# The loads of w1, 32 x 512 KB, are issued from ScalarE's DMA queue instead of SyncE's

## Chip, cores and metric

The kernel runs on one core of a Trainium2 chip. The metric is device time in microseconds (us); less is better. A core has five engines that each work through their own list of instructions: TensorE (PE), VectorE (DVE), ScalarE (ACT), GpSimd (POOL) and SyncE (SP), which here does nothing but issue loads and stores. They wait for one another by semaphores. A load is issued by an engine's sequencer (written SPq or ACTq in the profile) and moved by 16 DMA engines.

## What is computed

Three stages, float32. Windowed attention over 4 x 8 heads, 576 positions, head size 64, of which each position sees itself and the 63 before it; its result as 2304 tokens of 512; a soft mixture of 8 experts with 4 slots each; and a layer with softplus.

```python
scores = scale * np.matmul(q, k.transpose(0, 1, 3, 2))
mask = (rel >= 0) & (rel < window)                 # window = 64
x = softmax(scores where mask) @ v                 # 2304 x 512
...
logits = x @ phi                                   # 2304 x 32 slots
d = np.exp(logits - logits.max(0)); d /= d.sum(0) + 1e-09
slot_input = d.T @ x                               # 8 experts x 4 slots x 512
h = np.maximum(slot_input[e] @ w1[e], 0.0)         # w1: 8 x 512 x 1024
slot_out[e] = h @ w2[e]                            # w2: 8 x 1024 x 512
c = np.exp(logits - logits.max(1)); c /= c.sum(1) + 1e-09
x = c @ slot_out
...
h = x @ w_in                                       # 512 x 2048
g = np.maximum(h, 0.0) + np.log1p(np.exp(-np.abs(h)))
return g @ w_out                                   # 2048 x 512
```

## The kernel before

**Attention.** The 2304 tokens are 18 tiles of 128. Each tile t has a load of q (`do_lq`), of k (`do_lk`) and of v (`do_lv`), 256, 256 and 260 KB, into rings of four buffers. TensorE makes the scores (S, L227), VectorE masks them and finds the maxima (T, L238), GpSimd subtracts (M, L245), ScalarE takes exponentials (E, L248), TensorE transposes (PT, L254), ScalarE or VectorE copies the transposes out of PSUM (PC, by `evac`, L195), TensorE multiplies with v (PV, L272), VectorE normalises. Every four tiles the logits are made and folded into a running softmax over the tokens; ScalarE's part of that begins with the copy `lt` (L314).

**Weights.** w1 is 32 tiles of 128 x 1024 floats, 512 KB each, loaded by `load_w1` (L144 to L147) into 32 buffers that no one used before, so no load of w1 waits for a buffer. They are needed when the attention is over, by the first expert layer (`emit_l1`, L582). w2 is 32 more such tiles for the second expert layer (`emit_l2`, L625), loaded by `load_w2` (L156): the first four into space that the q and k buffers leave (`do_cl`, after the scores of the last tile), seven into what the other attention buffers leave, the rest into buffers of w1 as the first expert layer has used them. Behind w2 come w_in and w_out in halves of the last layer (L693, L696), which runs from about 130 us to the end.

**What sets the order.** A planner in the program, `arrange`, gets a table of steps with costs, dependencies and due times, and emits their instructions in the order that it finds. Loads are steps of the planned engine Q:

```python
step_1(("LQ", t), dict(Q=0.67), [("S", t - NQB)])
step_1(("LK", t), dict(Q=0.67), [("S", t - NKB + 1)])
step_1(("LV", t), dict(Q=0.67), [("PV", 2 * (t - NVB) + 1), ("VD", t - NVB + 1)])
...
step_1(("LW", j), dict(Q=1.31), [("LW", j - 1)], goal=100.0)
...
step_1(("CL", n), dict(Q=0.01), [("S", 17), ("LW", N1 - 1)] if n == 0 else [("PV", 35), ("CL", 0), ("VD", 17)])
```

So w1 (LW) is laid between the loads of q, k and v, two per tile, with a late due time. In the emitted program each engine keeps the order of emission. All loads share eight completion semaphores, DMAHW0 to DMAHW7, handed out in turn in the order of the program whatever engine issues; a load waits until the previous user of its semaphore, eight loads earlier, has landed. At the beginning ScalarE issues two loads itself, the first k tile and the constants.

Of the kernel before, what the change touches and what calls it, by code (L numbers as in the profile page):

```python
# [27 lines left out]
NWC0, NWC1 = 4, 7  # L28
NLAST, NEARLY = 2, 1
NWC = NWC0 + NWC1 + 3  # L30

# [72 lines left out]
def block_kernel(ctx: ExitStack, tc: tile.TileContext, q, k, v, phi, w1, w2, w_in, w_out, cst, out):  # L106
    nc = tc.nc
# [14 lines left out]
    def wtile(name):  # L122
        n_wt[0] += 1
        return (odd[n_wt[0] // 2 % 16] if n_wt[0] % 2 else wpa).tile([128, 1024], F32, tag="w", name=name)
# [18 lines left out]

    def load_w1(e, kt):  # L144
        t = wtile("w1t")
        nc.sync.dma_start(out=t, in_=w1[e, 128 * kt:128 * kt + 128, :])
        w_tiles["w1", e, kt] = t  # L147

    def load_w2(j, ts=None):
# [61 lines left out]
    def do_w1(e, j):  # L211
        load_w1(*w1_order[j])
# [338 lines left out]
    with tc.manual_schedule():  # L551
# [17 lines left out]
        l1_ps, h1_t, ring = {}, {}, {}  # L569
        takers = [NWC, "hTz0", NWC + 1, "hTz1"] + list(range(NWC + 2, NWC + 8))  # L570
        takers += [NWC + 8, "cc0", NWC + 9, "cc1", NWC + 10, "cc2"] + list(range(NWC + 11, N2 - NLAST))
        takers += [None] * (32 - len(takers))
# [30 lines left out]
        def emit_h1t(grp):  # L603
            h1 = h1_t.pop(grp)
            for hh in range(2):
                pst = bank(4 + hh, "ht_ps")
                for f in range(4):
                    base = h1[hh][:, 256 * (f // 2) + f % 2:256 * (f // 2) + f % 2 + 1]
                    rows = bass.AP(tensor=base.tensor, offset=base.offset, ap=[list(base.ap[0]), [2, 128]])
                    nc.tensor.transpose(pst[:, 128 * f:128 * f + 128], rows, ident)  # L610
                for e2 in range(2):
                    c0 = 16 * grp + 72 * e2
                    src0 = pst[:, c0:c0 + 1]
                    src = bass.AP(tensor=src0.tensor, offset=src0.offset, ap=[list(src0.ap[0]), [128, 4], [36, 2], [1, 4]])
                    dst0 = hTz[2 * grp + e2][:, 0, 4 * hh, 16 * grp + 8 * e2:16 * grp + 8 * e2 + 1]
                    dst = bass.AP(tensor=dst0.tensor, offset=dst0.offset, ap=[list(dst0.ap[0]), [NS, 4], [8 * NS + 4, 2], [1, 4]])
                    nc.vector.tensor_copy(dst, src)
# [3 lines left out]
        def emit_l2(j):  # L621
            e, r = w2_order[j]
            if r % 2:
                for g in range(4):
                    nc.tensor.matmul(  # L625
                        l2_ps[32 * g:32 * g + 32, :], hTz[e // 2][:, e % 2, 2 * r - 2 + g, :],
                        w_tiles["w2", j - 1 + g // 2][g % 2],
                        start=e == 0 and r == 1, stop=e == NE - 1 and r == 3,
                    )
# [16 lines left out]
        for i in range(4):  # L646
            t = ring[f"hTz{i // 2}"][:, 512 * (i % 2):512 * (i % 2) + 512]
# [25 lines left out]
        emit_h1t(1)  # L673
        for j in range(8, NWC):
            emit_l2(j)
# [52 lines left out]

        for j in range(NWC, N2):
            emit_l2(j)  # L730
            b, odd_j = divmod(j - NWC - 3, 2)
            if not odd_j and 0 <= b < 5:
# [288 lines left out]
```

## Time and profile before

| | us |
|---|---|
| median of 3 runs (lowest, highest) | 376.08 (375.13, 377.34) |
| the profiled execution, device time | 374.22 |
| its span, first to last instruction | 372.4 |
| TensorE busy | 361.5 (97%) |
| VectorE, ScalarE, GpSimd busy | 274.3, 236.7, 91.8 |
| moved on q1 (SP's queue) | 69.09 MB |
| moved on q10 (ScalarE's queue) | 0.66 MB |

The profile is one execution, a little shorter than the median run. Busy time is a share over stages with different limits, so the rows further down are taken by stage: attention until about 90 us, the expert layers until about 130 us, the last layer after that. In rows of the trace an arrow `out<-in` names what an instruction writes and reads, and `x2` counts instructions that one row stands for.

### The profile page before, as it was taken

What the parts mean: (1) busy time and instruction counts of PE and PEld (TensorE: products, weight loads), DVE (VectorE), ACT (ScalarE), POOL (GpSimd) and SP (SyncE); (2) the same over time, 40 slices, a digit from 0 to 9 for tenths busy, and PEclk for the clock granted to TensorE, in tenths of its full rate; (3) what the DMA queues carried; (4) which work ended last, traced back from release to release, by engine and by line L of the source; (5) the groups of instructions that cost most, each with busy time, mean ns of one, the idle gap of its engine ahead of it and who ended that gap; (6) DMA issues with size and microseconds to landing.
All of it is one profiled execution on the core that took longest, in us unless ns stands there. A gap on an engine that the chain in (4) does not pass through costs nothing.

```text
span 372.4 us, 8154 instructions
## 1 busy us (share of the span) xinstructions
PE 361.5 (97%) x3026; PEld 267.9 (72%) x3026; DVE 274.3 (74%) x777; ACT 236.7 (64%) x463; POOL 91.8 (25%) x111
## 2 busy tenths in 40 slices
PE   8999999998999998999999999999999999999995
PEld 6887878775333275887788878887768887878884
DVE  2786878845430399899998889989999885766562
ACT  1577665664200169888996687888778936666660
POOL 1999777730310001221000110122400100001230
PEclk9999999999999999999999999999999999999999
DMA  8999999999999994225330133141100030200222
GB/s 300 325 388 395 397 393 398 405 406 407 398 410 404 391 345 149 89 64 163 120 114 2 56 116 111 37 134 56 56 2 0 2 114 0 94 21 33 80 87 84
DMA packets 31096, 70.27 MB, mean 189 GB/s; under 512 B 2768, under 2 KB 11088, under 8 KB 31056
## 3 DMA queue, kind: packets, MB, share of 16 engines
q1 hardware_dynamic: 30768, 69.09, 50.4%
q10 hardware_dynamic: 288, 0.66, 0.5%
q8 instruction: 24, 0.39, 0.4%
q14 instruction: 16, 0.13, 0.1%
HBM read 65.02 MB, written 4.72 MB: 187 GB/s over the span
## 4 chain that ended last, share of the span: by engine, by line
PE 86%; DVE 5%; DMA 3%; ACT 2%; POOL 2%; issue 1%; DVEq 0%; POOLq 0%
PE y_ps L875 18%; PE y_ps L876 18%; PE y_ps L877 18%; PE x_ps L272 5%; PE s_ps L227 4%; PE pt_ps L254 4%; PE l_ps L582 4%; DMA w2t<-w_d 3%; PE x_ps L846 3%; PE xt_ps L295 2%; PE l_ps L625 2%; PE h_ps L846 2%; POOL sm L245 1%; PE lt_ps L305 1%; PE warm_ps L140 1%
## 5 line engine op out<-in xcount | busy, mean ns | idle before, releaser
L875 PE MATMUL y_ps<-whi,gh 128*128 128x512 f32 x288 | 115.1, 400 | 0.4 <-DVE part L886 0.3
L876 PE MATMUL y_ps<-wlo,gh 128*128 128x512 f32 x288 | 114.4, 397 | 0.0
L877 PE MATMUL y_ps<-whi,gl 128*128 128x512 f32 x288 | 113.7, 395 | 0.4 <-DVE gl L765 0.4
L765 POOL TENSOR_TENSOR gl<-g,gh 128x384 fp32r<-128x384 f32 (+2 forms) x24 | 26.9, 1119 | 225.0 <-DVE gh L762 126.5
L875 PEld LDWEIGHTS y_ps<-whi,gh 128*128 128x128 f32 x288 | 54.1, 188 | 16.5 <-issue 2.1
L877 PEld LDWEIGHTS y_ps<-whi,gl 128*128 128x128 f32 x288 | 54.1, 188 | 13.8 <-DVE gl L765 1.2
L876 PEld LDWEIGHTS y_ps<-wlo,gh 128*128 128x128 f32 x288 | 54.1, 188 | 11.1
L854 ACT ACTIVATE a<-a 128x512 f32<-128x512 f32 (+2 forms) x81 | 47.4, 585 | 2.6
L853 ACT ACTIVATE a<-a 128x512 f32<-128x512 f32 (+2 forms) x81 | 47.4, 586 | 1.5
L238 DVE CUSTOM_DVE_ANT_0 sm<-s_ps,cst_sb 128x128 f32<-128x128 f32 x144 | 32.8, 286 | 12.4 <-PE s_ps L227 8.9
L245 POOL TENSOR_TENSOR sm<-mx,sm 128x512 f32<-128x512 f32 x36 | 36.9, 1036 | 15.8 <-DVE mx L238 11.3
L765 DVE TENSOR_TENSOR gl<-g,gh 128x512 fp32r<-128x512 f32 (+1 forms) x57 | 36.9, 648 | 2.5 <-ACT gh L762 0.6
L849 ACT ACTIVATE a<-x_ps 128x512 f32<-128x512 f32 (+2 forms) x50 | 27.1, 547 | 16.4 <-PE x_ps L846 12.9
L858 DVE SCALAR_TENSOR_TENSOR g<-x_ps,a 128x512 f32<-128x512 f32 (+2 forms) x50 | 31.3, 627 | 7.3 <-ACT a L854 2.9
L762 DVE CAST gh<-g 128x512 fp32r<-128x512 f32 (+2 forms) x59 | 23.1, 391 | 13.9 <-PE y_ps L876 13.3
L248 ACT ACTIVATE sm<-sm 128x512 f32<-128x512 f32 x36 | 22.6, 634 | 16.9 <-POOL sm L245 16.3
L849 ACT ACTIVATE a<-h_ps 128x512 f32<-128x512 f32 (+1 forms) x31 | 16.9, 550 | 21.1 <-PE h_ps L846 21.1
L195 ACT COPY pt<-pt_ps 128x512 f32<-128x512 f32 x33 | 18.4, 584 | 6.8 <-PE pt_ps L254 6.7
L858 DVE SCALAR_TENSOR_TENSOR g<-h_ps,a 128x512 f32<-128x512 f32 (+1 forms) x31 | 19.6, 633 | 4.1 <-ACT a L854 3.4
L272 PE MATMUL x_ps<-vd,pt 128*64 128x65 f32 x288 | 21.6, 225 | 0.7 <-DVE xn L287 0.4
L272 PEld LDWEIGHTS x_ps<-vd,pt 128*64 128x64 f32 x288 | 18.5, 137 | 4.8 <-issue 3.1
L272 PE MATMUL x_ps<-vt,pt 128*64 128x65 f32 x288 | 21.7, 226 | 0.0
(143 smaller groups left out, 537.7 us busy)
## 6 DMA issues: line engine op xcount, KB each, us to landing
w1t<-w_d SPq DMA_DIRECT2D x32, 512.0 KB, 7.5
w2t<-w_d SPq DMA_DIRECT2D x29, 512.0 KB, 10.2
wi<-w_in_d SPq DMA_DIRECT2D x16, 512.0 KB, 5.3
wo<-w_out_d SPq DMA_DIRECT2D x16, 512.0 KB, 3.5
vt<-v_d SPq DMA_DIRECT2D x18, 260.0 KB, 6.0
qb<-q_d SPq DMA_DIRECT2D x18, 256.0 KB, 5.7
out_d<-o SPq DMA_DIRECT2D x18, 256.0 KB, 2.0
kr<-k_d SPq DMA_DIRECT2D x17, 256.0 KB, 5.8
```

Source lines behind the costliest of these rows:

```text
L238: nc.vector.tensor_tensor_reduce(out=sm[:, p], in0=ps[:, 128 * p:128 * p + 128], in1=mask, scale=-0.125, scalar=3.0e38, op0=ALU.add, op1=A ...
L245: nc.gpsimd.tensor_tensor(out=sm_t[i], in0=mb, in1=sm_t[i], op=ALU.subtract)
L272: nc.tensor.matmul(x_ps[64 * par:64 * par + 64, a, 65 * p:65 * p + 65], pt[:, 128 * p + 64 * par:128 * p + 64 * par + 64], vt[:, 65 * h:65 ...
L762: (nc.scalar.copy if e == "A" else nc.vector.tensor_copy)(dst, src)
L765: eng[e].tensor_tensor(out=dst, in0=a, in1=b.bitcast(F32), op=ALU.subtract)
L849: nc.scalar.activation(out=st["a", i], in_=st["h", i], func=AF.Abs)
L853: nc.scalar.activation(out=a, in_=a, func=AF.Exp, scale=-1.0)
L854: nc.scalar.activation(out=a, in_=a, func=AF.Ln, bias=1.0)
L858: nc.vector.scalar_tensor_tensor(out=st["g", i], in0=st["h", i], scalar=0.0, in1=st["a", i], op0=ALU.max, op1=ALU.add)
L875: nc.tensor.matmul(y, st["gh", i][:, ts], hi, start=first, stop=False)
L876: nc.tensor.matmul(y, st["gh", i][:, ts], lo, start=False, stop=False)
L877: nc.tensor.matmul(y, st["gl", i][:, ts], hi, start=False, stop=last)
```

## The change

One line: the issuing engine in `load_w1`. The planner's table is untouched, so it still counts the loads as steps of Q, and the loads are emitted where it puts them, now into ScalarE's list. Both halves of w1, all 32 loads, go through this line.

```diff
     def load_w1(e, kt):
         t = wtile("w1t")
-        nc.sync.dma_start(out=t, in_=w1[e, 128 * kt:128 * kt + 128, :])
+        nc.scalar.dma_start(out=t, in_=w1[e, 128 * kt:128 * kt + 128, :])
         w_tiles["w1", e, kt] = t
```

(A blank line is added further up, so lines after it have a number one higher in the changed kernel.)

In these lists `w1t`, `w2t`, `vt` are load targets of w1, w2 and v; `sm` is a tile of exponentials, `pt` and `xt` are copies of transposes, `lt` a copy of logits; the number behind a name tells tiles apart. The first place is ScalarE in mid-attention, in the changed program:

```order
L147 DMA w1t_1167<-w1_d 128x1024 [waits DMAHW5_49]
L196 COPY xt_1206<-xt_ps_1184 128x512 [waits PE_49]
L196 COPY dn_1227<-dt_ps_1197 128x128 [waits PE_49]
L196 COPY lnat_73<-dt_ps_1197 128x128
L147 DMA w1t_1233<-w1_d 128x1024 [waits DMAHW0_49]
L249 ACTIVATE sm_1150<-sm_1150 128x512 [waits Pool_49]
L196 COPY pt_1246<-pt_ps_1236 128x512 [waits PE_49]
L249 ACTIVATE sm_1169<-sm_1169 128x512 [waits Pool_49]
L147 DMA w1t_1264<-w1_d 128x1024 [waits DMAHW2_49]
L249 ACTIVATE sm_1200<-sm_1200 128x512 [waits Pool_49]
L196 COPY xt_1284<-xt_ps_1257 128x512 [waits PE_49]
L147 DMA w1t_1286<-w1_d 128x1024 [waits DMAHW5_49]
```

Before, this list had no loads; now w1t_1286 waits for DMAHW5, which w1t_1167 holds, and the next row behind it is the exponential sm_1248. The second place is the end of the attention. SP before:

```order
L209 DMA vt_1573<-v_d 128x520 [waits DMAHW7_49,PE_49,Pool_49]
L146 DMA w1t_1590<-w1_d 128x1024 [waits DMAHW0_49]
L146 DMA w1t_1608<-w1_d 128x1024 [waits DMAHW1_49]
L146 DMA w1t_1637<-w1_d 128x1024 [waits DMAHW2_49]
L146 DMA w1t_1670<-w1_d 128x1024 [waits DMAHW3_49]
L146 DMA w1t_1693<-w1_d 128x1024 [waits DMAHW4_49]
L146 DMA w1t_1717<-w1_d 128x1024 [waits DMAHW5_49]
L146 DMA w1t_1735<-w1_d 128x1024 [waits DMAHW6_49]
L146 DMA w1t_1755<-w1_d 128x1024 [waits DMAHW7_49]
L156 DMA w2t_1784<-w2_d 128x1024 [waits DMAHW0_49]
L156 DMA w2t_1788<-w2_d 128x1024 [waits DMAHW1_49,PE_49]
L156 DMA w2t_1792<-w2_d 128x1024 [waits DMAHW2_49]
```

SP now, at the same place (a load into reused space waits for several; the semaphores that the four w2 loads take in their turn are DMAHW2, DMAHW3, DMAHW5 and DMAHW7):

```order
L210 DMA vt_1501<-v_d 128x520 [waits DMAHW2_49,DMAHW3_49,PE_49,Pool_49]
L210 DMA vt_1573<-v_d 128x520 [waits DMAHW7_49,PE_49,Pool_49]
L157 DMA w2t_1784<-w2_d 128x1024 [waits DMAHW5_49,DMAHW2_49]
L157 DMA w2t_1788<-w2_d 128x1024 [waits DMAHW4_49,DMAHW3_49,PE_49]
L157 DMA w2t_1792<-w2_d 128x1024 [waits DMAHW6_49,DMAHW5_49,DMAHW1_49]
L157 DMA w2t_1796<-w2_d 128x1024 [waits DMAHW7_49]
L157 DMA w2t_1890<-w2_d 128x1024 [waits DMAHW4_49,PE_49,Activation_49]
```

The eight loads of w1 have gone from SP, so four loads of w2 follow the last v directly, and have moved ahead of most of these w1 loads in the turn of the semaphores. ScalarE now, at the same place:

```order
L147 DMA w1t_1637<-w1_d 128x1024 [waits DMAHW4_49]
L196 COPY xt_1659<-xt_ps_1639 128x512 [waits PE_49]
L147 DMA w1t_1670<-w1_d 128x1024 [waits DMAHW6_49]
L249 ACTIVATE sm_1628<-sm_1628 128x512 [waits Pool_49]
L196 COPY pt_1691<-pt_ps_1673 128x512 [waits PE_49,Activation_49]
L147 DMA w1t_1693<-w1_d 128x1024 [waits DMAHW0_49]
L196 COPY pt_1695<-pt_ps_1681 128x512 [waits PE_49,Activation_49]
L249 ACTIVATE sm_1645<-sm_1645 128x512 [waits Pool_49]
L147 DMA w1t_1717<-w1_d 128x1024 [waits DMAHW1_49]
L196 COPY xt_1728<-xt_ps_1712 128x512 [waits PE_49]
L147 DMA w1t_1735<-w1_d 128x1024 [waits DMAHW2_49]
L249 ACTIVATE sm_1697<-sm_1697 128x512 [waits Pool_49]
```

w1t_1590 and w1t_1608 still hold DMAHW0 and DMAHW1, for which w1t_1693 and w1t_1717 wait; w1t_1735 now waits for DMAHW2, which is w2t_1784's, and w1t_1755, three rows further down, for DMAHW3, which is w2t_1788's. Between them stand the exponentials and copies of the attention's last tiles.

## Rows read from the trace of the kernel before

**Rows 1.** The page, 40 slices of 9.3 us: DMA share in tenths, GB/s moved.

```profile
DMA  8999999999999994225330133141100030200222
GB/s 300 325 388 395 397 393 398 405 406 407 398 410 404 391 345 149 89 64 163 120 114 2 56 116 111 37 134 56 56 2 0 2 114 0 94 21 33 80 87 84
```

**Rows 2.** Windows: busy us (x instructions) of each engine, PEclk, DMA share, GB/s.

```profile
core 0: us, PE busy (x) PEld busy (x) DVE busy (x) ACT busy (x) POOL busy (x), PEclk, DMA share, GB/s
10.00:20.00 10.00, 9.61 (x217) 8.03 (x214) 8.04 (x62) 6.37 (x12) 9.66 (x12) 1.00 0.96 323
20.00:70.00 50.00, 50.00 (x1006) 40.35 (x1002) 40.14 (x238) 32.80 (x71) 40.02 (x50) 1.00 1.04 396
70.00:80.00 10.00, 9.34 (x168) 7.78 (x164) 5.84 (x32) 7.62 (x14) 6.97 (x9) 1.00 1.03 406
77.40:91.00 13.60, 12.61 (x222) 9.30 (x219) 6.40 (x22) 7.48 (x23) 1.10 (x2) 1.00 1.03 408
118.60:129.30 10.70, 9.77 (x76) 3.10 (x73) 3.62 (x6) 1.54 (x3) 0.00 (x0) 1.00 1.03 392
```

**Rows 3.** Chain of waits, 110 to 133 us: start, us, what.

```profile
118.58 10.64 DMA w2t<-w_d
129.27 1.08 PE l_ps L625 x4
```

**Rows 4.** SP, issues of w2 in time: start, us; then the landing of the last.

```profile
77.42 0.33 SPq L156 DMA_DIRECT2D w2t<-w_d  x1
...
78.60 0.33 SPq L156 DMA_DIRECT2D w2t<-w_d  x1
...
79.83 0.33 SPq L156 DMA_DIRECT2D w2t<-w_d  x1
...
82.45 0.33 SPq L156 DMA_DIRECT2D w2t<-w_d  x1
...
w2t<-w_d SPq DMA_DIRECT2D x1, 512.0 KB, 10.1
```

**Rows 5.** The page, DMA issues and queues: KB each, us from issue to landing; packets, MB.

```profile
wo<-w_out_d SPq DMA_DIRECT2D x16, 512.0 KB, 3.5
...
q10 hardware_dynamic: 288, 0.66, 0.5%
```

**Rows 6.** The tile w1t, its issues on SP: ns min/median/max, first and last start.

```profile
L146 SPq DMA_DIRECT2D w1t<-w_d x32: 327/428/1396, 15.9 to 75.4; - x32
```

**Rows 7.** ScalarE and its sequencer (ACTq) at the start of the kernel.

```profile
0.73 1.28 ACT L552 ACT_TABLE_LOAD   x1 [0.73 <-PEq L1009]
...
1.18 0.45 ACTq L556 DMA_DIRECT2D cst_sb<-cst_d  x1
```

**Rows 8.** One load of w1 on SP and its landing; a ScalarE instruction of 56 us.

```profile
L146 SPq DMA_DIRECT2D w1t<-w_d x1: 430/430/430, 50.6 to 50.6; - x1
...
DMA to landing us min/median/max: 6.5/6.5/6.5
...
56.27 0.63 ACT L248 ACTIVATE sm<-sm 128x512 f32<-128x512 f32 x1
```

**Rows 9.** ScalarE from 75 to 83 us, in time: start, us, what.

```profile
75.05 0.59 ACT L195 COPY pt<-pt_ps 128x512 f32<-128x512 f32 x1
...
76.56 0.59 ACT L195 COPY xt<-xt_ps 128x512 f32<-128x512 f32 x1 [0.39 <-PE xt_ps L295]
77.18 0.63 ACT L248 ACTIVATE sm<-sm 128x512 f32<-128x512 f32 x1
...
82.30 0.27 ACT L314 COPY lt<-lt_ps 128x128 f32<-128x128 f32 x1 [0.35 <-PE lt_ps L305]
```

**Rows 10.** DMA queues from 4 to 6 us; windows 4 to 6 and 6 to 8 us.

```profile
q1 hardware_dynamic: 230, 0.42, 55.7%
q10 hardware_dynamic: 141, 0.38, 48.6%
...
4.00:6.00 2.00, 2.00 (x25) 1.47 (x27) 0.00 (x0) 0.00 (x0) 0.00 (x0) 1.00 1.04 402
6.00:8.00 2.00, 1.87 (x31) 1.21 (x24) 1.14 (x11) 0.00 (x0) 0.12 (x1) 1.00 1.01 386
```

## The prediction

> **What bounds the kernel now.** I read the page's slices first: the 16 DMA engines are at nine tenths or more from slice 2 to slice 15, about 140 us, and carry some 400 GB/s there [rows 1]. TensorE is nearly full in the same time (50.00 of 50 us between 20 and 70 us) [rows 2], so two limits lie over each other, and the chain of waits says which ends last: it runs along TensorE until 118.58 us, stands 10.64 us on a load of w2, and goes on at 129.27 us [rows 3]. Up to 129 us the kernel is a stream of loads, and TensorE comes to its end 10.6 us early. The windows show how full that stream is: a DMA share of 1.03 or 1.04 in each, 408 GB/s where only 512 KB loads run, 396 in the attention, and a lower 0.96 only between 10 and 20 us [rows 2]. The change moves none of its bytes.
>
> Why it is gapless: a load waits for the one eight places ahead of it in the program, whose completion semaphore it uses again (the eight DMAHW names in the order above). In the trace this is SP's gait after 77 us: issues at 77.42, 78.60 and 79.83 us, one per 1.2 or 1.3 us, each when a load has landed, and each about 10 us ahead of its own landing, as the row of the issue at 82.45 has it [rows 4]. An unqueued 512 KB load takes 3.5 us (w_out, late in the kernel) [rows 5], so some 6.6 us of waiting work stands in the queue.
>
> **The change, part by part.**
> *Issue on SP:* 32 issues of 0.428 us [rows 6] leave SP, 13.7 us. SP is no compute engine and what ends its waits in this stretch is landings and freed buffers. Worth nothing: the 10 us of queue covers it.
>
> *Issue on ScalarE:* the same 13.7 us arrive there. Between 20 and 70 us ScalarE is busy 32.8 of 50 us [rows 2]; by their places in ScalarE's list 23 of the issues fall there, 9.8 us, in sum 42.6 of 50, so it fits even if none of it is hidden. Of the two loads that ScalarE issues already, the second went out at 1.18 us, under the table load of 0.73 to 2.01 us [rows 7], so an issue can lie beside a running instruction. From 70 to 80 us ScalarE is busy 7.62 us [rows 2] and gets seven issues, 3.0 us: 0.6 us too much if nothing is hidden, none if it is. I take none and keep 0.6 for the range.
>
> *The waits on ScalarE:* this is the new cost. Behind each w1 load stand exponentials and PSUM evacuations that TensorE needs, and the load waits for the landing eight places ahead. I put the landings of the trace beside the start of the ScalarE instruction that will stand behind the load. In mid-attention the tightest is w1t_1286: it waits for w1t_1167, which went out at 50.6 and took 6.5 us, so it landed at 57.1, and the exponential behind ran at 56.27 [rows 8]: held 0.8 us. At the end of the attention it tightens. w1t_1693 waits for w1t_1590, which had landed when SP issued at 77.42; the copy behind ran at 75.05: 2.37. w1t_1717 waits for w1t_1608, 78.60; the copy behind ran at 76.56: 2.04. w1t_1735 now waits for w2t_1784, which stands ahead of it and takes the place in the stream that landed at 79.83; the exponential behind ran at 77.18: 2.65 [rows 4, 9]. These are moments of one clock, so they don't add while the stream keeps its pace: ScalarE ends the attention late by the largest, 2.65 + 0.43 for the issue [rows 6] = **3.1 us**. Bounds: below, 0, if ScalarE's loads go out early enough to land before they are needed. Above, four w2 loads now go beside w1 from SP; if all four passed ahead of w1t_1608, it would land 4 x 1.28 = 5.1 us later (512 KB at 408 GB/s is 1.28 us), and the copy behind w1t_1717 would start at 78.60 + 5.1 + 0.43 = 84.1 instead of 76.56: 7.6 us late. That the queues share rather than follow each other is seen between 4 and 6 us, 0.42 MB on q1 beside 0.38 on q10 [rows 10], so the truth lies between 3.1 and 7.6, nearer the first since w1 keeps its half.
>
> *What that delay costs:* it moves TensorE, which has 10.64 us to spare [rows 3], and it moves the moment at which SP may load w2 into buffers that the attention frees. The first such load waits for ScalarE's copy lt, at 82.30 us; it was issued at 82.45 and landed 10.1 us later, at 92.6 [rows 4, 9]. With 3.5 us unqueued it could go out as late as 89.1: **6.6 us of slack**. So 3.1 us cost nothing, 7.6 us cost 1.0.
>
> *The stream itself:* the same bytes, on q10 beside q1 instead of all on q1. Rows of both kinds: with both queues 402 GB/s (4 to 6 us), with q1 alone 386 in the two microseconds after it [rows 10]. By these rows a mixture would be 4% better, 2.0 us over the 50 us of attention; I bound the loss by the lowest late stretch, 392 against 396 [rows 2], 0.5 us, and take 0, since the mixed window is flattered by the constants, whose rows are 3 KB long against 2 KB in q and k.
>
> The Trainium skill, "DMA: Bandwidth & Descriptors", section "Issuing engines are not separate DMA queues", holds that loads issued from several engines run on the same 16 DMA engines and that only the issue time is saved; its list for kernel authors says that spreading them for bandwidth doesn't help. By that the term is 0 and not 2.0 us; the trace, with its one mixed window, leans the other way without settling it, and the faster case below would lose its main piece.
>
> **Sum:** 0 (SP) + 0 (ScalarE's issue) + 0 (3.1 us late, under 6.6) + 0 (rate) = no change. The profiled execution took 374.22 us, 1.8 of it outside its span of 372.4; the median of the runs is 376.08, 1.9 above it. I set the forecast against the median: 376.1 us.
>
> **The rivals.**
> *Slower: ScalarE is held past the slack.* The three pieces add instead of hiding: 7.6 us with w2 ahead, 0.6 us of unhidden issue, and the hold in mid-attention with its issue, 0.8 + 0.43 = 1.2 us, that TensorE can't win back where it has no idle time [rows 2]. That is 9.4 us, the place is the copy lt, and from 6.6 us on each microsecond is paid by the stream running dry: 2.8 us, 378.9 us. For it: ScalarE works in order, and three loads are held already at the old landings. Against it: w1 keeps half of the DMA engines, and all else must go wrong together. From 10.6 us on TensorE's own arrival would pay too.
>
> *Faster: the stream runs quicker.* If two queues bring the attention's 396 GB/s to the 408 of pure 512 KB loads, 50 us shrink by 1.5 us; and w1 no longer stands behind SP's waits for freed buffers, which could fill the 0.08 of DMA share that 10 to 20 us lacks against the next stretch [rows 2], 0.8 us. Together 2.3 us, 373.8 us. Against it: those 396 are at a DMA share of 1.04, as busy as at 408.
>
> *The change does nothing it says.* The title speaks of the first layer's weights; the edited line is run for all 32 loads, and the order shows them on ACT. If both lists fed one hardware queue, nothing would be shared and the time would be the same; but the page has ScalarE's two loads on a queue of their own, q10 with 0.66 MB [rows 5], so I give this 2%, within the forecast's.
>
> **How the numbers follow.** A measurement of this kernel can tell about 0.5%, 1.9 us, from no change. No change: 58%, with a range of its own of 375 to 377.5. Slower: 26%, since that mechanism hangs on a wait whose length no row shows with both queues full. Faster: 16%. The range takes in both rivals' times with the scatter of the runs (375.13 to 377.34 now): 373.7 to 379.3 us.
>
> **What would show it.** q10 carries about 17 MB. The last w2 still lands at about 129 us and the chain of waits still shows a stand on w2, shortened from 10.6 us by ScalarE's delay (I expect 7 to 8 us left). The copy lt comes at 85 to 86 us. w1 loads take longer from issue to landing, q, k and v less. ScalarE's instructions near 75 us show waits for a DMA. The forecast is wrong if the copy lt comes after 89 us and DMA shows a gap near 90 us, or if the stand on w2 ends more than 1.9 us from 129.3 us.

## The result, and the profile after

The changed kernel takes 378.55 us (median of 8 runs, 377.29 to 380.52); the kernel before, run beside it, 375.04 us (8 runs, 374.17 to 377.34). The ratio is 1.0097, with a 95% interval of 1.0079 to 1.0115: slower by 0.97%, 3.5 us. The forecast of 376.1 us had the time within its range, but its likeliest case, no change, did not come; the time is near that of the slower rival. The profiled execution of the changed kernel took 378.65 us with a span of 376.8, 4.4 us more than the span of before, and that difference is what the traces below have to explain.

The queues do what the diff says. From the page after, the two rows of the 40 slices that answer to [rows 1], and the two queues that answer to [rows 5]:

```profile
DMA  8999999999999994333521133051200030200222
GB/s 287 347 355 360 324 399 400 389 409 408 401 404 409 392 354 129 111 113 94 182 62 56 56 113 111 1 170 37 75 3 0 1 113 0 83 30 28 84 86 83
...
q1 hardware_dynamic: 26160, 52.31, 39.0%
q10 hardware_dynamic: 4896, 17.43, 11.9%
```

ScalarE's queue q10 went from 0.66 to 17.43 MB: 32 loads of 512 KB more. The slices 3 to 5 carry 355, 360 and 324 GB/s, where they had 388, 395 and 397. The windows that answer to [rows 2], of the kernel after (same columns):

```profile
10.00:20.00 10.00, 9.61 (x217) 8.05 (x215) 8.03 (x63) 6.36 (x12) 9.68 (x12) 1.00 0.99 346
20.00:70.00 50.00, 46.77 (x930) 37.92 (x924) 36.09 (x215) 30.48 (x63) 37.45 (x46) 1.00 1.00 370
70.00:80.00 10.00, 9.26 (x172) 7.00 (x173) 8.96 (x52) 6.09 (x15) 6.84 (x10) 1.00 1.03 397
77.40:91.00 13.60, 10.80 (x195) 8.74 (x191) 5.75 (x27) 7.72 (x17) 5.16 (x7) 1.00 1.03 409
118.60:129.30 10.70, 10.25 (x84) 4.03 (x84) 1.27 (x5) 0.78 (x2) 0.00 (x0) 1.00 1.03 397
```

Two things are lost. In 20 to 70 us the stream moved 370 GB/s instead of 396, and TensorE was busy 46.77 of 50 us instead of all of them; from 77.4 to 91 us the stream is full (409) but TensorE is busy 10.80 us instead of 12.61. The chain of waits, whose rows of before were [rows 3], now ends its loads otherwise (start, us, what):

```profile
120.89 4.43 PE l_ps L626 x40
125.32 0.59 PE c_ps L737 x4
125.91 1.00 PE l_ps L626 x8
126.90 0.59 PE c_ps L737 x4
127.49 0.99 PE l_ps L626 x8
128.48 0.59 PE c_ps L737 x4
129.07 1.04 PE l_ps L626 x8
130.13 6.94 DMA wi<-w_in_d
```

No piece for w2 is left at the end: TensorE itself is last, matmul behind matmul. The load of w_in, with which the shown rows end, set nothing: the copy `so`, which follows the last matmul of the second expert layer, starts at 130.37 us before and at 134.79 after, and from there to the end it is the same 242 us:

```profile
130.37 0.37 ACT L762 COPY so<-l_ps 128x256 f32<-128x256 f32 x1 [4.52 <-PE l_ps L625]
```

```profile
134.79 0.37 ACT L763 COPY so<-l_ps 128x256 f32<-128x256 f32 x1 [2.37 <-PE l_ps L626]
```

ScalarE's view shows its new waits. From its timeline after, the five instructions that waited for a DMA between 56 and 89 us, and before the last three of them the loads at which it stood (ACTq is its sequencer); the last row, the copy lt, answers to [rows 9]:

```profile
57.87 0.63 ACT L249 ACTIVATE sm<-sm 128x512 f32<-128x512 f32 x1 [1.80 <-DMA qb<-q_d]
...
68.91 0.27 ACT L315 COPY lt<-lt_ps 128x128 f32<-128x128 f32 x1 [0.64 <-DMA qb<-q_d]
...
78.14 0.33 ACTq L147 DMA_DIRECT2D w1t<-w_d  x1
78.52 0.63 ACT L249 ACTIVATE sm<-sm 128x512 f32<-128x512 f32 x1 [0.78 <-DMA w1t<-w_d]
...
80.48 0.33 ACTq L147 DMA_DIRECT2D w1t<-w_d  x1
80.91 0.58 ACT L196 COPY pt<-pt_ps 128x512 f32<-128x512 f32 x1 [1.28 <-DMA w1t<-w_d]
...
83.02 0.34 ACTq L147 DMA_DIRECT2D w1t<-w_d  x1
83.40 0.58 ACT L196 COPY xt<-xt_ps 128x512 f32<-128x512 f32 x1 [1.38 <-DMA w1t<-w_d]
...
88.88 0.27 ACT L315 COPY lt<-lt_ps 128x128 f32<-128x128 f32 x1 [0.35 <-PE lt_ps L306]
```

The number in brackets is ScalarE's idle time and what ended it. At 78.14, 80.48 and 83.02 us a w1 load waited for an earlier w1 load to land, which left ScalarE idle for 0.78, 1.28 and 1.38 us; at two earlier w1 loads, issued at 57.49 and 68.53 us, it waited for loads of q, 1.80 and 0.64 us. The last copy lt stands at 88.88 instead of 82.30, 6.58 us late.

**Where the end comes from.** The matmuls of the two expert layers, in the tile view of l_ps, first for before and then for after (first and last start behind the comma):

```profile
L582 PE MATMUL l_ps<-w1t,siT x128: 592/592/617, 92.6 to 108.4; 128*32 128x512 f32 x128
L625 PE MATMUL l_ps<-w2t,hTz x128: 592/592/617, 108.8 to 129.7; 128*32 128x512 f32 x128
```

```profile
L583 PE MATMUL l_ps<-w1t,siT x128: 592/592/617, 99.2 to 115.0; 128*32 128x512 f32 x128
L626 PE MATMUL l_ps<-w2t,hTz x128: 592/592/617, 115.4 to 134.1; 128*32 128x512 f32 x128
```

Before, this stretch took 37.1 us from its first to its last matmul; after, 34.9, though it started 6.58 us later (99.20 against 92.62, by the chains). Windows over just that stretch, before and after:

```profile
92.62:129.73 37.11, 35.30 (x292) 11.82 (x292) 12.04 (x36) 4.62 (x11) 4.14 (x9) 1.00 1.03 401
```

```profile
99.20:134.14 34.94, 34.05 (x292) 11.78 (x292) 11.95 (x36) 4.63 (x11) 4.12 (x9) 1.00 1.04 399
```

34.94 us is what TensorE needs for these 292 matmuls with no wait for a load; before, it had 37.11 - 34.94 = **2.17 us** to spare, and no more. So the end is set by the later of two: the first layer's start, whose delay costs all but 2.17 us, and the landing of the last w2 (129.22 before). After: 6.58 - 2.17 = 4.41 us by the first, 3.39 us by the second (landing at 132.61). The larger is the 4.4 us of the spans.

### The profile page after: what moved, and what is told of

Read it like the earlier page. It is cut to its first block, busy times and chain, and to the rows that moved or that the text cites. A ratio compares the mean times of both kernels' runs of the same rounds, so it can differ in the third digit from the quotient of the medians.

```text
span 376.8 us, 8154 instructions
## 1 busy us (share of the span) xinstructions
PE 361.4 (96%) x3026; PEld 268.1 (71%) x3026; DVE 274.4 (73%) x777; ACT 236.5 (63%) x463; POOL 91.7 (24%) x111
## 3 DMA queue, kind: packets, MB, share of 16 engines
q10 hardware_dynamic: 4896, 17.43, 11.9%
## 4 chain that ended last, share of the span: by engine, by line
PE 75%; DMA 15%; DVE 4%; issue 2%; POOL 1%; ACT 1%; ACTq 0%; SPq 0%; DVEq 0%; POOLq 0%
PE y_ps L876 18%; PE y_ps L877 18%; PE y_ps L878 17%; DMA w1t<-w_d 6%; DMA w2t<-w_d 3%; PE l_ps L626 3%; PE x_ps L273 3%; PE s_ps L228 3%; PE x_ps L847 3%; PE pt_ps L255 2%; DMA qb<-q_d 2%; DMA kr<-k_d 2%; DMA wi<-w_in_d 2%; PE h_ps L847 2%; PE xt_ps L296 1%
## 5 line engine op out<-in xcount | busy, mean ns | idle before, releaser
L255 PE MATMUL pt_ps<-cst_sb,sm 128*128 128x128 f32 x144 | 21.3, 281 | 1.9 <-ACT xt L196 1.9
```

The source lines that it names most:

```text
L255: nc.tensor.transpose(ps[:, 128 * p:128 * p + 128], sm[:, p], ident)
```

## The experiments

Every profiled execution was read in the same two places. The first two columns are differences to the kernel before (first layer's start, last w2's landing, us); the third is the larger of (first - 2.17) and the second; the fourth is the span less 372.4:

| kernel | layer 1 starts | last w2 lands | by the rule | span |
|---|---|---|---|---|
| changed kernel | +6.58 | +3.39 | +4.41 | +4.4 |
| e1, again | +8.72 | +2.85 | +6.55 | +6.6 |
| e2, first 16 | +1.81 | +1.82 | +1.82 | +1.8 |
| e12, first 16 again | +2.19 | +1.74 | +1.74 | +1.8 |
| e3, last 16 | +4.23 | +0.27 | +2.06 | +2.1 |
| e4, k on ScalarE | +2.51 | +2.27 | +2.27 | +2.3 |
| e5, first 27 | +2.37 | +0.67 | +0.67 | +0.7 |
| e9, last 5 | +1.91 | -0.34 | -0.26 | -0.2 |
| e6, 16 copies | +6.15 | +0.33 | +3.98 | +3.9 |
| e7, 32 copies | +11.21 | +6.21 | +9.04 | +9.1 |
| e8, two early | +2.06 | -0.25 | -0.11 | -0.1 |
| e10, one early | +0.69 | -0.52 | -0.52 | -0.5 |
| e11, two early, later | +1.58 | -1.26 | -0.59 | -0.6 |

The rule holds within 0.15 us in all thirteen; the first row is no test of it, since the 2.17 us come from that execution. A profile is one execution, though, and the medians below don't always follow it.

**The changed kernel again.** No edit.

> The changed kernel once more, unaltered. Three theories of its 3.5 us: stream (two queues whose loads mix in mid-attention move fewer bytes per us), hold (ScalarE stands at the waits of the w1 loads, so the attention ends later), and stalls (TensorE's instruction fetches, 1.39 and 1.16 us, came late in that one execution). Stream: 378 to 379 us, and the queues of all loads again move 310 to 360 GB/s between 25 and 45 us. Hold: 378 to 379 us, the copy lt again near 88.9, whatever the rate in 25 to 45 us. Stalls: the rate in 25 to 45 us is above 380 GB/s in this profile, or the stalls lie elsewhere.

Measured: 377.82 us, ratio 1.0093 (1.0065 to 1.0122). The profiled execution is the longest of the six (380.79 us); the copy lt comes at 91.0. Between 25 and 50 us the queues move 372 GB/s, so the dip is there again, smaller. The stalls of TensorE are there again too, 1.27 us at 21.54 us, as in the first profile, and 1.02 us at 59.73 us, a new place, so they don't belong to that one execution; the place of the second is what the theory of stalls allowed for. What made this one long is in ScalarE's timeline and in the windows (PEclk, the third column from the right, is TensorE's granted clock):

```profile
80.92 0.59 ACT L196 COPY pt<-pt_ps 128x512 f32<-128x512 f32 x1 [3.17 <-DMA w1t<-w_d]
```

```profile
78.00:82.00 4.00, 1.56 (x34) 1.26 (x34) 0.52 (x6) 1.08 (x2) 1.67 (x3) 1.00 1.03 411
82.00:84.00 2.00, 0.96 (x15) 0.66 (x10) 1.06 (x3) 0.81 (x3) 1.23 (x2) 0.80 1.04 414
84.00:88.00 4.00, 4.00 (x41) 3.25 (x42) 0.03 (x1) 2.00 (x4) 0.00 (x0) 0.50 1.03 410
88.00:90.00 2.00, 2.00 (x16) 1.65 (x20) 1.03 (x3) 0.67 (x2) 0.00 (x0) 0.50 1.04 412
90.00:92.00 2.00, 2.00 (x65) 1.73 (x57) 0.45 (x2) 0.87 (x3) 0.00 (x0) 0.99 1.00 397
```

ScalarE stood 3.17 us at one w1 load, TensorE was busy 1.56 of 4 us, and then its clock was granted at 0.50 (1.2 GHz) from 84 to 90 us. What that cost shows against the first profile, whose clock stood at 1.00 there. The same four matmuls, behind the same copy xt, in the first profile and then in this one:

```profile
84.03 0.66 PE L255 MATMUL pt_ps<-cst_sb,sm 128*128 128x128 f32 x4 [1.22 <-ACT xt L196]
```

```profile
83.87 1.12 PE L255 MATMUL pt_ps<-cst_sb,sm 128*128 128x128 f32 x4 [1.03 <-ACT xt L196]
```

From there to the first layer's start it is 15.17 us in the first profile (to 99.20) and 17.47 in the second (to 101.34): 2.3 us more with the fallen clock, which covers the difference of the two delays in the table (8.72 and 6.58). So the hold has a second price, paid by TensorE after the wait is over.

**The first 16 loads only, the last 16 only.**

```
eng = nc.scalar if w1_order.index((e, kt)) < 16 else nc.sync     # e2; ">= 16" in e3
eng.dma_start(out=t, in_=w1[e, 128 * kt:128 * kt + 128, :])
```

> Only the first 16 of the 32 w1 loads are on ScalarE's queue (issued up to some 58 us), the last 16 on SyncE's. Stream: as slow as the changed kernel, 378 us, last w2 landing near 132. Hold: the late waits (0.6 to 1.8 us each after 57 us) are back on SyncE, so 375 to 376 us, copy lt back near 82 to 84.

> Only the last 16 of the w1 loads are on ScalarE's queue (issued from some 58 us on). Stream: 375 to 375.5 us, over 385 GB/s in 25 to 45 us, last w2 landing near 129.2. Hold: 377.5 to 379 us, with ScalarE standing at the last w1 loads and the copy lt at 86 to 89.

Measured: the first 16, 374.44 us, 1.0001 (0.9983 to 1.0019). The last 16, 377.38 us, 1.0067 (1.0044 to 1.009), with the last w2 at 129.49, lt at 86.5, ScalarE idle 1.59, 1.26 and 1.57 us at w1 loads (before 58.00, 78.35 and 81.04 us), and 397 GB/s between 25 and 50 us. That speaks for the hold: the late half carries 2.6 of the 3.0 to 3.5 us, and it does so without any loss in the stream.

**The first 27 loads only, the last five only.** The same edit with `< 27` and `>= 27`.

> The first 27 of the w1 loads are on ScalarE's queue, the last five on SyncE's: those five are the ones at which ScalarE stood (0.8 to 3.2 us each, 76 to 85 us) for a load eight places earlier to land. Hold: the first layer starts before 95 us and the time is 374.5 to 376 us. Stream (the mix of queues costs the time): 377 to 378.5 us, since nearly all of w1 still comes by the second queue.

> Only the last five w1 loads are on ScalarE's queue, the other 27 on SyncE's, so no queues mix before 75 us. Hold: these five carry nearly the whole cost, the first layer starts 96.5 to 99 us and the time is 377 to 378.5 us. If the cost were spread over all 32 loads: 375 to 375.5 us.

Measured: the first 27, 374.81 us, 1.0002 (0.9979 to 1.0025): 27 of the 32 loads can be on ScalarE at no cost that the interval shows. It isn't that none of them waits: in this profile too ScalarE is idle 1.69 us before 53.40 us, at a w1 load that waits for a load of q, and 0.60 us before 59.12. The last five alone, 375.81 us, 1.0035 (1.001 to 1.006), which is 0.4 to 2.2 us and not the 2.3 to 3.8 expected. The table shows why the parts don't add to the whole: each delays the first layer by about the slack (2.37 and 1.91 us), and only what goes beyond 2.17 us counts; all 32 delay it by 6.58 and 8.72 us, far beyond it and more than the two parts together. The executions of the last five sort by TensorE's granted clock: spans of 371.6 to 373.2 us in the four with a mean clock of 0.997 or more, 373.3 to 375.3 in the six at 0.993 to 0.995, 375.8 in one at 0.989. That order speaks for the fallen clock as the main cost there; it isn't shown, since their traces were not taken.

**A delay without any queue.** In the kernel before, the last lt copy is done 16 or 32 times more:

```
-        nc.scalar.copy(lt, ps_t.pop(("lg", b))[:, 0:128])
+        ps = ps_t.pop(("lg", b))
+        for _ in range(17 if b == 3 else 1):     # 33 in e7
+            nc.scalar.copy(lt, ps[:, 0:128])
```

> The kernel before with the last lt copy done 17 times instead of once: 16 x 0.266 = 4.3 us more on ScalarE at the end of the attention, and no queue is touched. ScalarE stands idle some 2 us there, so the first layer starts 2 to 2.5 us later (94.6 to 95.1). Small slack (TensorE stood idle only 2.2 us between the first layer's start and the last w2): 0 to +0.5 us, 375 to 375.5 us. Large slack (TensorE can give 10 us): 0, 374.8 us.

> As the run with 16 copies, with 32 more: 8.5 us on ScalarE, so the first layer starts 6 to 6.7 us later, as in the changed kernel (99.2). Small slack: the end moves by that less 2.2 us, so +4.1 to +4.5 us, 379 us, more where TensorE's clock falls while it waits. Large slack: +0 to +0.3 us, 375 us.

Measured: 378.8 us, 1.0106 (1.0077 to 1.0135), and 383.9 us, 1.0236 (1.021 to 1.0261). I missed the delay of the first layer (6.15 and 11.21 us instead of 2 to 2.5 and 6 to 6.7), but not the rule: from those delays less 2.17 us follow 3.98 and 9.04, and the medians moved by 4.0 and 9.1. Large slack is refuted; a ScalarE that is merely late, with every load on its old queue, costs as much as the change. Windows of the run with 32 copies say why the delay is longer than the copies, and that the stretch itself is the same 34.95 us:

```profile
84.00:92.00 8.00, 0.54 (x4) 0.30 (x4) 0.00 (x0) 7.14 (x28) 0.00 (x0) 0.70 1.02 407
92.00:96.00 4.00, 2.52 (x13) 1.72 (x17) 1.84 (x8) 2.76 (x10) 0.00 (x0) 0.50 1.03 410
...
103.83:138.78 34.95, 34.05 (x292) 11.79 (x292) 11.96 (x36) 4.63 (x11) 4.13 (x9) 1.00 0.94 354
```

TensorE does 0.54 us of work in eight, and comes back at half its clock.

**Another pair of queues.** w1 is on SyncE again, the loads of k on ScalarE:

```
-        (nc.sync if e == "Q" else nc.scalar).dma_start(out=kr[:, t % NKB], in_=k[t])
+        nc.scalar.dma_start(out=kr[:, t % NKB], in_=k[t])
```

> w1 is back on SyncE's queue; instead the 17 loads of k (4.4 MB, 0.25 MB each) are issued by ScalarE's. Stream: two queues mix again from 5 to 70 us, so below 375 GB/s in 25 to 45 us and 377 to 379 us. Hold: ScalarE now waits at the k loads for TensorE's scores instead of for w1, so the copy lt moves by what those waits cost, and the time is 375 to 377 us with the stream at 390 GB/s.

Measured: 375.97 us, 1.0037 (1.0019 to 1.0055), 386 GB/s between 25 and 50 us, lt at 84.8. Inconclusive between the two theories: its profile ends by the last w2 (+2.27 us), but of the 0.8 MB that it lacks at 50 us 0.6 were lost before 25 us.

**The dip once more.** The kernel with the first 16 loads, a second profile.

> The kernel with the first 16 w1 loads on ScalarE's queue, one more profile: in the first the queues moved 342 to 370 GB/s between 25 and 50 us, and 0.74 MB were missing at 50 us, while its median time was that of the kernel before. If the dip belongs to some executions only: over 380 GB/s there in this one and a span near 372.4 us. If it belongs to two queues: 340 to 370 GB/s again, with a span near 374.

Measured: a span of 374.2 and the dip again, as in the first profile. Windows from 25 to 50 us of five kernels: before; after; the first 16, first and second profile; the first 27:

```profile
25.00:50.00 25.00, 25.00 (x512) 20.51 (x509) 18.90 (x113) 17.21 (x37) 20.23 (x25) 1.00 1.04 396
```

```profile
25.00:50.00 25.00, 23.84 (x506) 19.56 (x498) 18.01 (x117) 16.41 (x34) 18.73 (x24) 1.00 0.97 347
```

```profile
25.00:50.00 25.00, 24.10 (x492) 19.81 (x489) 17.79 (x112) 15.99 (x33) 18.93 (x24) 1.00 1.00 358
```

```profile
25.00:50.00 25.00, 25.00 (x518) 20.51 (x514) 18.70 (x117) 17.12 (x36) 19.97 (x25) 1.00 1.01 370
```

```profile
25.00:50.00 25.00, 24.69 (x504) 20.23 (x504) 18.38 (x112) 17.05 (x37) 20.34 (x25) 1.00 1.04 396
```

The kernels e3, e6, e7 and e9, with one queue in this stretch, move 392 to 397; e10, with one queue too, fell to 350 between 35 and 40 us. With w1 on the second queue it is 347 to 372 in four profiles of five, and 396 in one. So two queues often cost rate here, but not always; that the dip belongs to two queues as such isn't shown, since the kernel with the first 27 has two and no dip. A rival is left: the four profiles with a dip are also those in which TensorE stood 0.9 to 1.7 us at a time in mid-attention without a wait that the trace names (two such pieces in the changed kernel are shown further down), and the first 27 has no such piece above 0.4 us. (The kernels with early loads, further down, have them on one queue too, of some 0.5 us.) In two of the four TensorE was busy throughout the window shown (25.00 of 25 us), but had stood just ahead of it. Which of the two brings the other, no run here separates. What it costs in time is also open: both profiles of the first 16 are 1.8 us long, by the rule because of the late w2, but its twelve timed runs have the median of before; four of their spans lie at 373.7 to 374.4 us and eight at 371.8 to 372.9.

**A version that beats both.** In the kernel before, each w1 load is issued one or two places earlier, all on SyncE; the places gained are filled behind loads of q, in the stretch from 10 to 20 us in which the stream has room (323 GB/s) [rows 2]:

```
     def do_lq(e, t):
         nc.sync.dma_start(out=qb[t % NQB], in_=q[t])
+        if t in (4, 5):              # t == 5 in e10; (5, 6) in e11
+            do_w1("Q", 0)
...
+    n_w1 = [0]
+
     def do_w1(e, j):
-        load_w1(*w1_order[j])
+        if n_w1[0] < N1:
+            load_w1(*w1_order[n_w1[0]])
+            n_w1[0] += 1
```

> The kernel before with every w1 load issued two places earlier on SyncE's queue: the first two right behind the loads of q at 7.4 and 10.0 us, in the stretch in which the queues moved 286 to 353 GB/s. If the stream sets the end in the kernel before: the last w2 lands 0.7 to 2.0 us earlier and the time is 373 to 374.3 us, and no more than 2.2 us is to be had, since TensorE's path from the first layer's start is next. If the loads of q, k and v are only pushed back: the attention ends later and the time is 375 to 377 us.

> Every w1 load one place earlier on SyncE's queue (the first behind the load of q at 10.0 us) instead of two. The run with two moved the end by 1.3 us, and its first layer started 2.1 us later, since loads of k landed late. With one: the stream gains half (0.4 MB, 1.0 us) and the attention loses at most half (1 us, within the 2.2 us of slack): 373.3 to 374.3 us. If two was right for another reason than the bytes: 374.8 us.

> Two places earlier, as in the run with two, but the first two loads stand behind the loads of q at 10.0 and 12.0 us instead of 7.4 and 10.0 us, by which time the scores' loads are further ahead. If the late loads of k cost the attention there: the first layer starts before 94.5 us and the time is 372.5 to 373.6 us. If the place makes no difference: 373.5 us again.

Measured: 373.55 us, 0.9954 (0.9935 to 0.9972); 373.33 us, 0.9958 (0.9941 to 0.9976); 373.02 us, 0.995 (0.9931 to 0.9969). All three are faster than before by 0.4 to 0.5%; between them nothing can be told. The first profile doesn't show the gain: its last w2 lands 0.25 us earlier, not the 0.7 to 2.0 expected, and it is the slowest of its eight executions (374.06 us). Of the third, the windows that answer to [rows 2]:

```profile
10.00:20.00 10.00, 9.78 (x216) 8.24 (x215) 7.98 (x60) 6.36 (x13) 9.64 (x13) 1.00 1.06 393
20.00:70.00 50.00, 48.73 (x990) 39.69 (x988) 38.67 (x232) 31.95 (x68) 38.34 (x48) 1.00 1.04 397
118.60:129.30 10.70, 10.70 (x90) 3.44 (x82) 3.53 (x6) 1.54 (x3) 0.00 (x0) 1.00 1.04 388
```

10 to 20 us now carry 393 GB/s, 0.7 MB more than before, and in the last stretch TensorE has no idle time left: the next bound, as expected, is TensorE's 34.94 us from the first layer's start, which came 1.58 us later (94.20).

## Why the prediction was right or wrong

*Issue on SP, issue on ScalarE (0 and 0): right.* The 32 issues take 0.334 us (median) on ScalarE's sequencer (0.428 was reckoned [rows 6]) and stand beside running instructions: the load at 84.81 us goes out while the copies of 84.42 and 84.89 run on. The first 27 loads, 9.0 us of issue, cost nothing that the interval shows in the run with them alone.

*The waits on ScalarE (3.1 us, bounds 0 and 7.6): the mechanism right, the size below and the places in part wrong.* ScalarE was held at w1 loads for the reason given, and lt came 6.58 us late. Counted from the last load back, the loads at 80.48 and 83.02 us are w1t_1693 and w1t_1717, as said. The one at 78.14 us is w1t_1670, which I hadn't named, and w1t_1735, on whose 2.65 us the 3.1 rest, wasn't held: it went out at 83.42 us, behind w1t_1717. In mid-attention the hold of 1.80 us was at w1t_1233, not at w1t_1286. I took the landings from the trace of before, as "moments of one clock". They move: w1t_1608, for which w1t_1717 waits, went out at 75.11 us instead of 69.86, since ScalarE was late already, and landed at 83.00 instead of 78.54. So here a load that went out late made the next hold later.

Nor is all of the 6.58 us a hold. TensorE's scores, at about 50 us (from the chains, with the two pieces of the changed one) and for the last tile (from the timelines), first after and then before:

```profile
21.98 1.39 issue
...
35.07 1.16 issue
...
51.82 1.10 PE s_ps L228 x32
...
75.43 1.10 PE L228 MATMUL s_ps<-kr,qb 64*64 64x128 f32 x32
```

```profile
48.82 1.03 PE s_ps L227 x32
...
71.12 1.10 PE L227 MATMUL s_ps<-kr,qb 64*64 64x128 f32 x32
```

At 51.82 us TensorE is 3.0 us late, and 2.55 of them are the two pieces called "issue", in which it stood within a run of 32 matmuls. Nothing of them was foreseen. Their cause isn't shown, but the trace has a hint: queue q8, which the page of the profile calls "instruction", moves a 16 KB packet from 20.98 to 21.96 us and another from 33.95 to 34.96, where the kernel before has them start at 17.22 and 30.72; TensorE goes on 1.4 and 1.3 us after they end. Late instructions would fit that, but which engine a packet was for the trace doesn't say, and the second stall of the changed kernel's other profile (59.73 us) has no such packet right before it. Another 1.3 us came between 52 and 75 us, where ScalarE was held for the two loads of q, and the last 2.3 us at the three holds at the end. So the holds make some 3.6 us of it (an estimate, 1.3 + 2.3), near the 3.1. In executions without those two pieces the first layer was 1.9 us (last five) to 4.2 us (last 16) late.

*What that delay costs: this is the step that failed.* By it no change came out as the likeliest case. I wrote that the delay "moves TensorE, which has 10.64 us to spare [rows 3]", and that it is paid only beyond the 6.6 us of slack of the copy lt. The 10.64 us are a load, from its issue at 118.58 to its landing, that the chain follows back to SP; they are not idle time of TensorE. The window row beside it says so: from 118.6 to 129.3 us TensorE was busy 9.77 of 10.70 us [rows 2], with work for the loads that had landed already. The real slack is 2.17 us. With it even my own 3.1 us would have cost 0.9 us, and the measured 6.58 cost 4.41. The slack of lt was read rightly for what it is: with lt at 88.88, just inside the 89.1 that I named, the stream shows no gap near 90 us (409 GB/s from 77.4 to 91), and with lt at 92.4 (32 copies) it falls to 273 GB/s from 96 to 104 us. But TensorE's path comes due 4.4 us sooner.

*The stream's rate (0, bounds -2.0 and +0.5 us): wrong in the profiles, not on the path here.* 370 GB/s instead of 396 from 20 to 70 us made the last w2 land 3.39 us late, seven times the bound of the loss. It didn't set the end, since TensorE was later by 1.0 us. The gain of 2.0 us that the mixed window hinted at didn't come. That the Trainium skill, in "DMA: Bandwidth & Descriptors", section "Issuing engines are not separate DMA queues", saw no bandwidth to be won agrees with these 370 GB/s; a loss, which they also show, it doesn't speak of.

*The rivals.* Slower, at 378.9 us, was the case that came, by ScalarE being held. That its time is so near the 378.55 is partly luck: it was set against 376.08 us, and the kernel before measured 375.04 beside it, so as differences it is 2.8 us forecast and 3.5 measured; and its 9.4 us of delay, less 6.6, had little to do with the measured 6.58 less 2.17. The point from which it decides was taken as 6.6 us where 2.2 was true, and its payer was TensorE, not the stream. With the window read rightly, this would have been the likeliest case. The stated range is also narrower than its own words: both rivals' times with the scatter of the runs, 375.13 to 377.34 around 376.08, would be 372.9 to 380.2 us. Faster fell; its one sound piece is the gap from 10 to 20 us, worth 0.4 to 0.5% when the loads go there on SyncE's own queue. That the change does nothing is refuted by q10's 17.43 MB.

*What would show it.* I expected the last w2 at about 129 us, 7 to 8 us of stand left, lt at 85 to 86, and w1 longer in the queue: it was 132.61, none, 88.88, and 6.9 us for w1 where it had 7.5. ScalarE's waits for a DMA near 75 us came from 78 us on, and two came earlier, at 57 and 68 us. My sign that the forecast is wrong, a w2 more than 1.9 us from 129.3, did show.

**What stays open:** what makes the stream dip with two queues in most executions, what the "issue" pieces are and whether they come with the dip or make it, and how the 3.5 us of the median split between late ScalarE and fallen clock in the executions that were only timed.

## What to carry to other kernels

A DMA piece in the chain of waits is a load's way from issue to landing; before it is taken as an engine's slack, read the engine's busy time in that window, or the length of the stretch in an execution where nothing is waited for. A queue on an engine that computes makes its waits those of the work behind it: loads that seldom wait, early in a stage with slack behind it, may go there (27 of 32 here, though two of them held it 1.69 and 0.60 us), those that wait for a landing at the end of the stage cost time. Delays of several small causes cost nothing up to the slack and all of it beyond, so parts that are free alone need not be free together.

## What was not expected of the hardware

- A wait of 3 us on ScalarE left TensorE busy 1.56 of 4 us, and its granted clock then stood at 0.50 for some 6 us (changed kernel again, 84 to 90 us), 2.3 us of time against the profile in which it didn't fall; after 8 us with 0.54 us of work the same came in the run with 32 copies (0.50 from 92 to 96 us).
- Loads of 512 KB on a second queue beside loads of 256 KB on the first moved 347 to 372 GB/s in four profiles of five, at a DMA share of 0.97 to 1.02, against 386 to 397 at 1.03 or 1.04 on one queue; no window in [rows 10] or elsewhere in the trace of before had hinted at a loss.
